# Whole float32 scores in twelve heads instead of eight, and the high parts of V cast on ACT instead of GpSimd

## The chip, the cores and the metric

The kernel runs on one core of one Trainium2 chip. The metric is the device time of one execution in microseconds (us). The engines are named as the profile names them: PE is TensorE's matmul, PEld its weight load, DVE is VectorE, ACT is ScalarE, POOL is GpSimd, and SP issues the transfers.

## The reference

Eight batches of eight heads of attention (576 positions, 64 columns a head) with a mask in blocks of 64 positions, then a mixer: a product of rank 32 along the sequence added to the input, and a feed-forward layer of 512 to 2048 to 512 with a residual.

```python
scores = scale * np.matmul(q, k.transpose(0, 1, 3, 2))
mask = block_i >= block_j
scores = np.where(mask, scores, -1000000000.0)
scores = scores - np.max(scores, axis=-1, keepdims=True)
attn = np.exp(scores)
attn = attn / (np.sum(attn, axis=-1, keepdims=True) + 1e-09)
out = np.matmul(attn, v)
...
h = xt @ U @ V
u = x + h.transpose(0, 2, 1)
ch = np.maximum(u @ w_ch1, 0.0) @ w_ch2
return u + ch
```

All inputs and the output are float32.

## The kernel before

The 64 heads (number h, batch h // 8) pass through the same steps one after the other. `split_qk` fetches q and k of a head into a tile `raw` of 128 partitions: 64 hold q and k, and the other 64 hold a pattern that brings the mask into the product. `softmax` makes the scores of five row tiles (the last, 128 rows by 576 columns, in a double bank `bw`; the others in single banks), takes the row maximum on DVE (L949) and the exponential on ACT (L960). `normalise` multiplies by the inverse of the row sums on POOL (L986). `transpose` turns the probabilities on PE (L1019) and moves them out of PSUM, `apply_v` multiplies by V, and after every second head `mix` does the product of rank 32 and writes u to DRAM.

Two ways of computing stand beside each other, and a constant says how many heads go the first way.

- Scores. The first `FS` = 8 heads are whole: ACT scales k (L874), and one float32 product of `raw` with itself (L931) gives scores and mask. PE runs such a product at float32, and it shows as two MATMUL records each in the trace. The other heads are split: ACT casts q and k to float32r, a type whose products PE runs faster (L877 and L878), POOL and DVE form the rests (L880, L885), SP copies the high part of q into a second tile (q<-q, L892) and fetches q and k a second time into the other 64 partitions (L861), and two float32r products (L935, L936) are summed. In the last two of the whole heads DVE also copies the mask's pattern into the tiles of the split heads (L867).
- Probabilities times V. The first `FP` = 10 heads multiply in float32 (L1061). The others split probabilities and V into high and low parts (L996, L1038 and `split_v`) and multiply in float32r (L1077). In `split_v` POOL makes the high part (L904), then the low one (L907).

The weights of the feed-forward layer arrive as 64-bit words that ACT, DVE and POOL turn into float32 and split (`split64`, L331 to L361); this work is laid beside heads 0 to 17 or so. As soon as the first batch is through `mix`, the feed-forward products with the first half of the hidden columns (`ffn_chunk`, L465 and L488) fill PE between the steps of attention, in two banks `bf` of their own. After the last head they run alone, and the second half of the hidden columns follows (`block_products`, L659).

The order on each engine is made ahead of time: `Plan.issue` plays the tasks with an estimated cost each. A task has an engine, a cost in ns, a priority (a head's number times 1000 and a little more; filler has 1,000,000 and more), and the buffers that it reads and writes. Of the tasks whose inputs are there, the one with the lowest number is issued. Tasks on POOL and those marked `port` are never planned at the same time. What is issued stays in that order on its engine. A change of one cost, engine or task thus lays the whole order anew.

Of the kernel before, what the change touches and what calls it, by code (L numbers as in the profile page):

```python
# [13 lines left out]
ALU = mybir.AluOpType  # L14
# [29 lines left out]

FP = 10

FS = 8

PB = (1, 1, 1, 2, 2)

# [87 lines left out]
class Plan:  # L138
# [8 lines left out]
    def add(self, engine, ns, prio, fn, reads=(), writes=(), hold=(), after=0, port=False):  # L147

        n = len(self.tasks)
        deps = set()  # L150
        for b in reads:
            deps.update(b.writers)
            b.readers.append(n)
        for b in hold:
            deps.update(b.readers, b.writers)
        for b in writes:
            deps.update(b.readers, b.writers)
            b.writers, b.readers = [n], []
        deps.discard(n)
        slots = {b for b in (*reads, *writes) if b.pool is not None}  # L160
        for b in slots:
            b.users += 1
        self.tasks.append((engine, ns, prio, fn, deps, after, slots, port or engine == "POOL"))
# [76 lines left out]
def _act(n, sbuf=False):  # L240
    return (93 if sbuf else 52) + 0.833 * n
# [13 lines left out]
def attention_then_mixer(  # L255
# [10 lines left out]
    nc = tc.nc  # L266
# [10 lines left out]
    def f32(ap):  # L277
        return ap.bitcast(F32)
# [525 lines left out]
    for r in raw_r:  # L804
# [3 lines left out]
        for x, fill in ((qi, 1.0), (ki, NEG)):  # L808
            nc.gpsimd.affine_select(
                out=x[:, :, 1, :], in_=x[:, :, 1, :], pattern=[[-1, 4], [0, 64]], compare_op=ALU.not_equal,  # L810
# [44 lines left out]
    def split_qk(h, pr):  # L855
        raw, q1, k1, q2, k2 = (r[h % 2] for r in (raw_r, q1_r, k1_r, q2_r, k2_r))

        def fetch():
            nc.sync.dma_start(out=raw[0:64, :], in_=qk[h])
            if h >= FS:  # L860
                nc.sync.dma_start(out=raw[64:P, :], in_=qk[h])  # L861

        if h in (FS - 2, FS - 1):

            for n, (x, o) in enumerate(((q2, 0), (k2, S))):
# [3 lines left out]
                )  # L869
        add("SP", 1640 if h >= FS else 820, pr, fetch, writes=[raw], after=DL)  # L870
        if h < FS:
            add(
# [21 lines left out]
    def split_v(h, pr):  # L894
        s = h % 2
        raw, vs = vr_r[h // 2 % 2], vs_r[s]
        if s == 0:
            add("SP", 910, pr, lambda: nc.sync.dma_start(out=raw.ap, in_=v[h // 2]), writes=[raw], after=DL)
        if h < FP:
            return  # L900
        hi, lo = vs[:, :, 0:64], vs[:, :, 64:P]
        add(
            "POOL", 430, pr,
            lambda: nc.gpsimd.tensor_scalar(out=hi, in0=raw[:, s], scalar1=1.0, scalar2=1.0, op0=ALU.mult, op1=ALU.mult),  # L904
            [raw], [vs],
        )
        add("POOL", 820, pr, lambda: nc.gpsimd.tensor_sub(lo, raw[:, s], f32(hi)), [raw, vs], [vs])  # L907

    def softmax(h, tiles, pr):
# [14 lines left out]
        def products():  # L924
            for i, at in parts:
                qs = slice(P * i + 64 - (P if i else 64), P * i + 64)
                for j in range(2 if wide else 1):
                    o = bank[:, j, :T] if wide else view(i, at)
                    ks = slice(j * T, j * T + T) if wide else slice(0, P * i + 64)
                    if h < FS:  # L930
                        nc.tensor.matmul(  # L931
# [7 lines left out]
        for i in tiles:  # L939
            ns += [T] * 4 if wide else [P * i + 64] * 2  # L940
            ms += [P if i else 64] * (4 if wide else 2)
        if h < FS:
            add("PE", sum(1.667 * n for n in ns) / 2, pr, products, [raw], [bank])
# [207 lines left out]
    wa = weight_tiles(wp, 0)  # L1151
    split_qk(0, 0.0)
    split_v(0, 0.1)
    mixing_weights(MP)
    wab = weight_bufs()
    load_w1(lambda: wa, 0, wab, lambda n: WP0 + WP1 * n, (0,))
    for h in range(NH):
        pr = 1000.0 * h
        if h + 1 < NH:
            split_qk(h + 1, max(pr - LA, 1.0))  # L1160
        for g, tiles in ((1, (4, 3)), (0, (2, 1, 0))):
            for x in ((4,), (3,)) if g else ((2,), (1, 0)):
                softmax(h, x, pr + 10)
            normalise(h, tiles, pr + 10)
        for g in (1, 0):
            for part in range(2):
                transpose(h, g, part, pr + 20 + 10 * (1 - g))
            apply_v(h, g, pr + 30)
        if h + 1 < NH:
            split_v(h + 1, pr + 1000)  # L1170
        if h % 2 == 1:
            mix(h // 2, pr + 40)
        if h == min(WH, NH - 1):
            gate = Buf()
            gate.writers = [len(plan.tasks) - 1]
            load_w2(lambda: wa, 0, wab, lambda n: WPB + WP1 * n, [gate], ks=range(FH))
            load_w1(lambda: wa, 0, wab, lambda n: WP2 + WP3 * n, (1,), [gate])
            load_w2(lambda: wa, 0, wab, lambda n: WP4 + WP3 * (n - FH), [gate], ks=range(FH, FC))
# [59 lines left out]
```

## Time and profile before

| | |
|---|---|
| median of 3 runs | 1201.78 us (1198.8 to 1202.18) |
| the profiled execution | 1201.04 us |
| its span | 1199.2 us |
| PE, DVE, ACT, POOL busy | 1169.1, 980.7, 734.0, 426.3 us |
| first split product of scores (L935), last | 77.3 us, 659.4 us |
| first filler product (L465) | 103.5 us |

The span is what lies between the first and the last instruction of the profile. In a row of a timeline the first number is the start and the second the duration, in us from the span's start; in a group, busy time and mean duration stand before the second bar and the idle time ahead of its instructions, with what ended it, behind it. PE's matmuls are pipelined: the next one starts before the one before it ends, so a stretch of work is read from start to start.

### The profile page before, as it was taken

The page shows a single profiled execution, that of the slowest core. Times are in us where ns is not written, and L with a number is a line of the kernel's source. Part 1 is how long each engine was busy: PE and PEld are TensorE (multiplying, and loading weights), DVE is VectorE, ACT ScalarE, POOL GpSimd, SP SyncE. Part 2 cuts the span into 40 slices and gives each one's busy share as a digit, 9 for nine tenths or more (in the row PEclk, how much of TensorE's full clock was granted, in tenths as well). Part 3 has the DMA queues.
Part 4 walks back from the last instruction along what each step waited for, and adds up shares of the span by engine and source line. Part 5 has one row for each costly group of instructions (what it writes and reads, how often), then busy time and mean ns, then how long its engine had stood idle before and what let it go on. Part 6 is the DMA issues. An engine that isn't in the chain of part 4 may idle for free.

```text
span 1199.2 us, 25106 instructions
## 1 busy us (share of the span) xinstructions
PE 1169.1 (97%) x8970; PEld 1123.6 (94%) x8970; DVE 980.7 (82%) x2061; ACT 734.0 (61%) x1822; POOL 426.3 (36%) x588
## 2 busy tenths in 40 slices
PE   7989998999999999999999999999999999999998
PEld 5657888999999999999999999999999999999998
DVE  6879899888988898888887488425989889889887
ACT  6878686777878787878786344213544544544443
POOL 4558766665656566665654112210000000000000
PEclk9999999999999999999999999999999999999999
DMA  4465656535364535354532343211231231231221
GB/s 127 146 172 155 188 166 166 139 97 156 81 171 108 144 104 153 101 158 106 144 98 70 104 147 111 81 54 49 72 119 49 72 119 49 72 119 60 60 80 40
DMA packets 76428, 132.13 MB, mean 110 GB/s; under 512 B 9040, under 2 KB 53072, under 8 KB 76304
## 3 DMA queue, kind: packets, MB, share of 16 engines
q1 hardware_dynamic: 76304, 130.53, 38.8%
q8 instruction: 71, 1.16, 0.4%
q14 instruction: 53, 0.43, 0.1%
HBM read 92.75 MB, written 29.49 MB: 102 GB/s over the span
## 4 chain that ended last, share of the span: by engine, by line
PE 79%; DVE 11%; ACT 4%; issue 2%; DMA 2%; SPq 0%; POOL 0%; ACTq 0%; DVEq 0%; POOLq 0%
PE bb L659 29%; PE bf L465 10%; PE bf L488 10%; PE ba L1019 7%; PE ba L1077 5%; PE bg L465 4%; PE bg L488 4%; DVE mx L949 2%; DVE pl L1038 2%; ACT p L960 2%; PE ba L935 2%; PE ba L936 2%; PE ba L1061 1%; PE ba L1116 1%; PE ba L1102 1%
## 5 line engine op out<-in xcount | busy, mean ns | idle before, releaser
L986 POOL TENSOR_SCALAR p<-p,rv 128x192 f32<-128x192 f32 (+4 forms) x320 | 181.0, 580 | 150.5 <-DVE rv L977 92.7
L659 PE MATMUL bb<-hh,w1l 128*128 128x288 f32 x704 | 170.1, 295 | 0.0
L659 PE MATMUL bb<-hh,w1h 128*128 128x288 f32 x704 | 169.4, 295 | 0.0
L960 ACT ACTIVATE p<-ba,mx 128x448 f32<-128x448 f32 (+3 forms) x248 | 114.3, 466 | 22.2 <-DVE mx L949 18.9
L1019 PE MATMUL ba<-ident,p 128*128 128x128 f32 x768 | 123.5, 275 | 2.2 <-DVE pw L994 0.7
L1038 DVE TENSOR_TENSOR pl<-ba,ph 128x512 fp32r<-128x512 f32 x216 | 114.0, 550 | 11.7 <-ACT ph L996 9.2
L659 PE MATMUL bb<-hl,w1h 128*128 128x288 f32 x576 | 123.0, 295 | 0.1
L659 PEld LDWEIGHTS bb<-hh,w1l 128*128 128x128 f32 x704 | 122.9, 190 | 0.0
L659 PEld LDWEIGHTS bb<-hh,w1h 128*128 128x128 f32 x704 | 121.9, 188 | 0.0
L488 PE MATMUL bf<-hh,w2h 128*128 128x288 f32 x392 | 121.2, 309 | 0.0
L488 PE MATMUL bf<-hl,w2h 128*128 128x288 f32 x392 | 116.4, 297 | 0.0
L488 PE MATMUL bf<-hh,w2l 128*128 128x288 f32 x392 | 115.6, 295 | 0.0
L996 ACT CAST ph<-ba 128x512 fp32r<-128x512 f32 x216 | 100.5, 493 | 23.1 <-PE ba L1019 18.3
L447 POOL TENSOR_TENSOR ul<-ur,uh 128x288 fp32r<-128x288 f32 x72 | 63.3, 907 | 129.7 <-PE bf L465 72.6
L613 ACT CAST hh<-hb 128x576 fp32r<-128x576 f32 x98 | 65.9, 672 | 60.6 <-PE bb L659 58.1
L949 DVE TENSOR_REDUCE mx<-ba 128x1 f32<-128x448 f32 (+3 forms) x248 | 94.1, 407 | 10.0 <-PE ba L936 5.4
L1019 PEld LDWEIGHTS ba<-ident,p 128*128 128x128 f32 x768 | 90.5, 141 | 7.9 <-issue 4.5
L880 POOL TENSOR_TENSOR q<-raw,q 64x576 fp32r<-64x576 f32 x56 | 82.6, 1475 | 29.1 <-issue 9.2
L659 PEld LDWEIGHTS bb<-hl,w1h 128*128 128x128 f32 x576 | 91.9, 188 | 0.4 <-DVE hl L614 0.4
L1077 PE MATMUL ba<-ph,vs 128*128 128x256 f32 (+3 forms) x432 | 90.7, 263 | 0.1
L465 PE MATMUL bf<-uh,w1l 128*128 128x288 f32 x392 | 80.8, 303 | 0.0
L488 PEld LDWEIGHTS bf<-hh,w2l 128*128 128x128 f32 x392 | 74.9, 191 | 0.2
(167 smaller groups left out, 3288.1 us busy)
## 6 DMA issues: line engine op xcount, KB each, us to landing
raw<-in_qk_dram SPq DMA_DIRECT2D x120, 288.0 KB, 4.4
st<-in_w_dram SPq DMA_DIRECT2D x32, 512.0 KB, 3.6
o_d<-ot SPq DMA_DIRECT2D x72, 144.0 KB, 2.1
vr<-in_v_dram SPq DMA_DIRECT2D x32, 320.0 KB, 3.4
ur<-u_d SPq DMA_DIRECT2D x64, 144.0 KB, 3.0
whole<-o_d SPq DMA_DIRECT2D x32, 288.0 KB, 3.2
out_dram<-whole SPq DMA_DIRECT2D x32, 288.0 KB, 2.2
ur<-u_d SPq DMA_DIRECT2D x30, 288.0 KB, 3.2
```

Source lines behind the costliest of these rows:

```text
L465: nc.tensor.matmul(ps[:, :T], w()[wn][:, k, fs], m[k].ap, start=(i == 0), stop=(i == len(ops) - 1))
L488: nc.tensor.matmul(ps[:, :T], w()[wn][:, f, ms], hs[f][x].ap, start=(i == 0), stop=(i == len(ops) - 1))
L613: add("ACT", _act(2 * T, True), E, lambda: nc.scalar.copy(h.ap, x[0]()), [x[1]], [h])
L659: nc.tensor.matmul(bank[:, i, :T], x()[:, w(k)], p.ap[:, k, :], start=first and n == 0, stop=last and n == len(ops) - 1)
L880: "POOL", 1380, pr, lambda: nc.gpsimd.tensor_sub(q1[64:P, :], raw[64:P, 0:S], f32(q1[64:P, :])),
L949: lambda i=i, at=at: nc.vector.tensor_reduce(out=mx[: P if i else 64, i : i + 1], in_=view(i, at), op=ALU.max, axis=AX.XY if wide else AX. ...
L960: nc.scalar.activation(out.rearrange("p (j k) -> p j k", j=2) if wide else out, view(i, at), AF.Exp, bias=mx[:rows, i : i + 1], accum_out= ...
L986: lambda x=x, rows=rows, i=i: nc.gpsimd.tensor_scalar(out=x, in0=x, scalar1=rv[:rows, i : i + 1], scalar2=1.0, op0=ALU.mult, op1=ALU.mult),
L996: add("ACT", _act(n), pr, lambda: nc.scalar.copy(out(), inp()), reads, writes)
L1019: nc.tensor.transpose(out=bank[:, a : a + P], in_=pt_r[i][h % PB[i]][:, j * P : (j + 1) * P], identity=perm.ap)
L1038: "DVE", _dve(m), pr, lambda: nc.vector.tensor_sub(pl[:, low], bank[:, :m], f32(ph[:, low])), [bank, bh], [bl]
L1077: nc.tensor.matmul(bank[0 : c.stop, a:n], vs[:, j, c], x[:, _at(g, j)], start=(i == 0), stop=(i == len(ops) - 1))
```

## The change

`FS` becomes 12: heads 8 to 11 too compute their scores in one whole float32 product. For these four heads the casts L877 and L878, the rests L880 and L885, the copy L892 and the second fetch L861 fall away, and the scaling L874 comes in. The copies of the pattern (L867) move from heads 6 and 7 to heads 10 and 11. The row tile 3 of these heads' scores stays in the attention's own banks, since that choice goes by h < 8 and not by `FS`.

In `split_v` the high part of V is made by ACT (`nc.scalar.copy`, a cast to float32r) with a planned cost of `_act(320, True)`, 93 + 0.833 x 320 = 360 ns, in place of POOL's multiplication by one with 430 ns. This goes for the 54 heads from 10 to 63. The low part stays on POOL.

```diff
@@ -44,7 +44,7 @@
 FP = 10
 
-FS = 8
+FS = 12
 
@@ -900,8 +900,7 @@
         hi, lo = vs[:, :, 0:64], vs[:, :, 64:P]
         add(
-            "POOL", 430, pr,
-            lambda: nc.gpsimd.tensor_scalar(out=hi, in0=raw[:, s], scalar1=1.0, scalar2=1.0, op0=ALU.mult, op1=ALU.mult),
+            "ACT", _act(320, True), pr, lambda: nc.scalar.copy(hi, raw[:, s]),
             [raw], [vs],
         )
         add("POOL", 820, pr, lambda: nc.gpsimd.tensor_sub(lo, raw[:, s], f32(hi)), [raw, vs], [vs])
```

## The prediction

> **What bounds the kernel now.** I read the page first for the engine that is never free, then busy time by stretches of the span for where that engine is idle after all, and last the waits and the order of time in those stretches. On the page:
>
> ```profile
> span 1199.2 us, 25106 instructions
> PE 1169.1 (97%) x8970; PEld 1123.6 (94%) x8970; DVE 980.7 (82%) x2061; ACT 734.0 (61%) x1822; POOL 426.3 (36%) x588
> ```
>
> TensorE (PE) is busy in 1169.1 of 1199.2 us, 30.1 us short of the span. Attention has the higher priority, and the feed-forward products (L465, L488) fill what it leaves, so an attention step that gets slower merely hands its place on TensorE to filler. The time can move in two ways only: by the work given to TensorE, or by its idle time. Where that lies (columns: length; busy time and instructions of PE, PEld, DVE, ACT, POOL; granted clock; DMA share; GB/s):
>
> ```profile
> 10.00:66.00 56.00, 53.83 (x294) 36.03 (x293) 46.33 (x122) 45.71 (x130) 28.91 (x43) 1.00 0.48 138
> 66.00:104.00 38.00, 31.45 (x198) 22.38 (x197) 29.21 (x62) 30.81 (x84) 23.91 (x28) 1.00 0.64 168
> 104.00:200.00 96.00, 87.03 (x665) 82.09 (x664) 89.62 (x205) 71.27 (x196) 66.86 (x83) 0.95 0.59 166
> 200.00:660.00 460.00, 457.05 (x3777) 445.67 (x3777) 391.76 (x1017) 360.16 (x1032) 277.18 (x397) 1.00 0.47 124
> 122.00:128.00 6.00, 4.48 (x21) 4.26 (x22) 4.05 (x9) 1.68 (x5) 3.04 (x3) 0.72 0.31 102
> 178.00:186.00 8.00, 5.73 (x23) 4.58 (x24) 7.67 (x13) 3.98 (x11) 4.19 (x6) 0.57 0.61 176
> ```
>
> Idle TensorE by difference: 2.2 us of 56 while heads 0 to 7 run (4%); 6.5 us of 38 in 66-104, where heads 8 to 10 have split scores and no filler is ready yet; 9.0 us of 96 in 104-200, where DVE is 93% busy; 2.9 us of 460 after that. In two places the granted clock sinks too: 4.48 us of work at 0.72 and 5.73 at 0.57 cost 1.3 and 2.5 us, so 104-200 holds 12.7 us that could be had. The change touches the second and third rows.
>
> **The change part by part: the scores of heads 8 to 11.** Each gets one whole product in place of two split ones. TensorE in the order of time (start, duration), first a whole head, then a split one; the matmuls are pipelined, so the price is from a row's start to the next row's start:
>
> ```profile
> 49.62 1.39 PE L931 MATMUL ba<-raw 128*128 128x320 f32 x6
> 50.84 2.04 PE L1061 MATMUL ba<-pw,vr 128*64 128x256 f32 x10
> ...
> 53.93 1.14 PE L931 MATMUL bw<-raw 128*128 128x288 f32 x4
> 54.90 0.92 PE L931 MATMUL bf<-raw 128*128 128x448 f32 x2
> 55.65 0.27 PE L1102 MATMUL ba<-ident,xt 128*64 128x128 f32 x1
> ...
> 102.44 0.47 PE L935 MATMUL ba<-k,q 128*128 128x448 f32 x1
> ...
> 103.54 0.77 PE L465 MATMUL bf<-uh,w1h 128*128 128x288 f32 x4
> ...
> 105.78 0.38 PE L935 MATMUL bw<-k,q 128*128 128x288 f32 x1
> ...
> 106.39 0.70 PE L465 MATMUL bf<-uh,w1h 128*128 128x288 f32 x4
> ```
>
> Whole: 1.22 (50.84 - 49.62) + 0.97 + 0.75 = 2.94 us. Split: 1.10 + 0.61 = 1.71 us. That is 1.23 us more a head and **+4.9 us** for four, on the path because TensorE has no room elsewhere (4.6 to 5.2 if the starts are each off by a slot of 0.1).
>
> What leaves the other engines, by lines (duration in ns, lowest/median/highest):
>
> ```profile
> L877 ACT CAST q<-raw x56: 656/673/693, 69.4 to 630.6; 128x576 fp32r<-128x576 f32 x56
> L878 ACT ACTIVATE k<-raw x56: 667/686/711, 69.9 to 631.9; 128x576 fp32r<-128x576 f32 x56
> L880 POOL TENSOR_TENSOR q<-raw,q x56: 1396/1426/1993, 70.5 to 633.9; 64x576 fp32r<-64x576 f32 x56
> L885 DVE SCALAR_TENSOR_TENSOR k<-raw,k x56: 718/752/1910, 70.7 to 633.4; 64x576 fp32r<-64x576 f32 x56
> L874 ACT ACTIVATE raw<-raw x8: 669/682/686, 4.5 to 55.2; 64x576 f32<-64x576 f32 x8
> L892 SPq DMA_DIRECT2D q<-q x56: 482/489/1835, 72.3 to 636.4; - x56
> ```
>
> A head gives up two ACT passes for one (-0.68 us), 1.43 us of GpSimd, 0.75 of DVE, and on SP's queue the copy q<-q (L892) and the second fetch of q and k (L861). All of this runs beside TensorE, so it is worth nothing in itself. It counts in 66-104 through the waits:
>
> ```profile
> PE bw L936 <- DMA q<-q: 3.1, 1, 3.1
> 72.34 8.43 DMA q<-q
> DMA to landing us min/median/max: 2.3/3.0/8.4
> ```
>
> The first split head cannot start its second product until q<-q has landed, 8.4 us after issue, and TensorE stands for 3.1 us with nothing to fill. After the change this place belongs to a whole head. TensorE's order at head 8, before:
>
> ```order
> L1019 MATMUL ba_96<-ident,p_1_140 128x128 x2
> L935 MATMUL bw<-k_0_147,q_0_145 128x288
> L936 MATMUL bw<-k_0_128,q_0_126 128x288
> ```
>
> and in the changed program (it is a line shorter from L903 on, so L930 is the whole product, L934 and L935 the split one); first head 8, then, at "...", head 12, now the first split one:
>
> ```order
> L1101 MATMUL ba_96<-ident,xt_163 64x128
> L930 MATMUL bw<-raw_130 128x288 x2
> L1018 MATMUL ba_97<-ident,p_1_138 128x128
> ...
> L465 MATMUL bf_91<-ul_112,w1h_199 128x288
> L465 MATMUL bf_91<-ul_113,w1h_199 128x288
> L934 MATMUL bw<-k_0_147,q_0_145 128x288
> L935 MATMUL bw<-k_0_128,q_0_126 128x288
> ```
>
> Head 8 no longer needs a copy, and head 12 comes behind filler. I take 66-104 at the pace of the whole heads before it, 4% idle: 1.5 us in place of 6.5, **-5.0 us**. At best nothing stays idle (-6.5); at worst only the wait for q<-q goes (-3.1). The two casts a head of L867 (the rows that split heads reuse) move from heads 6 and 7 to 10 and 11; DVE has 8.8 us free in 66-104 and hides four casts of 1 us:
>
> ```profile
> L867 DVE CAST q<-raw x2: 685/1029/1373, 32.9 to 41.2; 64x576 fp32r<-64x576 f32 x2
> ```
>
> Without that cover the 4 us would come before the row maxima of heads 10 and 11, inside the worst case above.
>
> **The high parts of V.** 54 instructions go from GpSimd to ACT:
>
> ```profile
> L904 POOL TENSOR_SCALAR vs<-vr 128x320 fp32r<-128x320 f32 x54 | 24.8, 460 | 54.7 <-PE ba L1077 51.3 <-DMA raw<-in_qk_dram 2.0 <-ACT uh L445 0.6
> L445 ACT CAST uh<-ur 128x288 fp32r<-128x288 f32 x72 | 27.7, 432 | 2.8 <-PE bf L465 1.8 <-DVE ur L1136 0.6 <-PE bg L465 0.2
> L360 ACT CAST w1h<-z x8: 600/618/622, 32.5 to 131.5; 128x512 fp32r<-128x512 f32 x8
> L960 ACT ACTIVATE p<-ba,mx 128x448 f32<-128x448 f32 (+3 forms) x248 | 114.3, 466 | 22.2 <-DVE mx L949 18.9 <-DVE xt L1085 0.7 <-DVE rv L976 0.6
> ```
>
> ACT casts 288 columns in 0.432 us and 512 in 0.618, so 320 take about 0.46, 24.8 us in all, what GpSimd gives up. ACT is at 78% in 200-660 (360.16 of 460); some 46 casts (one in 10 us) add 21 us, 83%. That is cover enough for 0 on TensorE; bounds -1 and +3 us (its idle time there gone, or doubled). The cast waits for the P V products two heads back (L1077), and ACT's exponentials queue behind it. The changed order on ACT, at one of these casts (L1082 takes the product out of PSUM, L903 is the cast):
>
> ```order
> L1118 COPY tb_169<-ba_98 32x128
> L1082 COPY tmp_162<-ba_96 64x320
> L1120 CAST t_0_167<-tz_168 32x128
> L903 CAST vs_151<-vr_149 128x5x64
> L353 ACTIVATE z_103<-st_101 128x512
> ```
>
> The cast stands behind a copy that already waits for the last product reading that V, so it hardly adds a wait of its own.
>
> In 104-200 the lateness is DVE's, and some comes with GpSimd's work:
>
> ```profile
> L331 DVE TENSOR_SCALAR z<-z x36: 175/423/2499, 8.5 to 757.7; 128x512 f32<-128x512 f32 x32, 96x288 f32<-96x288 f32 x2, 128x128 f32<-128x128 f32 x1, 128x32 f32<-128x32 f32 x1
> 180.60 2.50 DVE L331 TENSOR_SCALAR z<-z 128x512 f32<-128x512 f32 x1
> 180.20 0.45 POOL L904 TENSOR_SCALAR vs<-vr 128x320 fp32r<-128x320 f32 x1
> 181.34 0.86 POOL L907 TENSOR_TENSOR vs<-vr,vs 128x320 fp32r<-128x320 f32 x1
> PE ba L1131 <- DVE xt L1085: 1.7, 1, 1.7
> ```
>
> An operation with a median of 0.42 us took 2.50 while GpSimd ran back to back, L904 among it, in the stretch where the clock sank. Some eight L904 leave this stage, 3.7 us of such meetings, and attention comes to it about one head further on. The order is laid out anew, though, so stalls may fall elsewhere. I take **-3 us** of the 12.7, a little less than the 3.7; bounds -12.7 (all) and +4.8 (one more stretch like 178-186: 2.3 idle and 2.5 of clock).
>
> [...]
>
> Sum: 4.9 - 5.0 - 3 + 0 = **-3.1 us**. The profiled execution took 1201.04 us (span 1199.2); the median of the runs is 0.7 above it, so the forecast is 1201.04 - 3.1 = 1197.9, and 1198.7 against the median; I give **1198.3**. All bounds together are -17.6 to +9.9.
>
> **The rivals.**
> *The stalls of 104-200 go.* If 9 of their 12.7 us vanish: 4.9 - 5.0 - 9 = -9.1, about 1192. For it: DVE works less and GpSimd's meetings fall. Against: DVE stays over 90%, since the weights still have to be split in this stage.
> *A draw.* The 66-104 gain pays for the heavier products and nothing else changes: 4.9 - 5.0 = -0.1, about 1201. For it: the two terms rest on the best rows; against: nothing says that the old stalls would come back unchanged.
> *Slower: the switch to split heads stalls at head 12.* The copy q<-q is late there too, since SP has fetches, weights and the filler's traffic in one queue: 3.1 us of wait and 2.5 of sunk clock: 4.9 - 5.0 + 3.1 + 2.5 = +5.5, about 1206.5. It decides once the copy lands later than the filler ahead of head 12 lasts. Against: 18 filler products stand shortly ahead of it in TensorE's order, and this copy took 3.0 us to land in the median.
>
> ACT's other exponentials, and TensorE's longest wait for them:
>
> ```profile
> L960 ACT ACTIVATE p<-bw,mx 128x576 f32<-128x576 f32 x64 | 47.5, 742 | 16.9 <-DVE mx L949 15.5 <-DVE rv L976 0.5
> PE ba L1019 <- ACT p L960: 2.8, 5, 1.4
> ```
>
> *ACT blocks.* The 51.3 us that L904 waited on GpSimd come to ACT's queue. Of ACT's own waits for the row maxima (18.9 + 15.5) TensorE saw 2.8 us, a twelfth; a twelfth of 51.3 is 4.2: -3.1 + 4.2 = +1.1, about 1202. [...]
>
> **How the numbers follow.** Forecast 0.42, stalls gone 0.15, draw 0.23, head 12 0.13, ACT 0.07. A measurement here can tell about 0.3% (3.6 us) from no change, so faster means under 1198.2. The forecast lies on that line: I give 0.23 of its 0.42 to faster and 0.19 to same, and 0.04 of the draw to faster. Faster 0.23 + 0.15 + 0.04 = 0.42; same 0.19 + 0.17 + 0.05 = 0.41; slower 0.13 + 0.02 (draw) + 0.02 (ACT) = 0.17. The range for 8 in 10 is 1191 to 1206, which takes in four of the cases and the near side of the slower one; the likeliest case alone has 1195 to 1201.
>
> **What would show it.** Right: idle TensorE in 66-104 under 2 us, no wait for q<-q at head 8, twelve heads of L930 at 2.9 us each, first filler no later than the 103.5 us of before, ACT at 83% in 200-660 with TensorE's idle time there still near 3 us. Wrong: a wait for q<-q or for the split k at head 12, waits of ACT on the P V products at L903, more idle time or more low clock in 104-200 than 12.7 us together, or 66-104 not above 92% busy.

## The result, and the profile after

The changed kernel takes 1188.71 us in the median of four runs (1185.44 to 1190.97), the kernel before, on the same chip, 1201.82 (1198.8 to 1202.18): a ratio of 0.989 with a 95% interval of 0.9859 to 0.992. That is 13.1 us less, where 3.1 us less was forecast (against the 1201.04 of the profiled execution), and 2.3 us below the lower end of the range. The profiled execution took 1186.6 us. Two of the four runs, the profiled one among them, took 1185.44 and 1186.6 us at a mean granted clock of 1.000, the other two 1190.83 and 1190.97 us at 0.997, so what the profile shows is the quicker kind.

The page of the changed kernel, its span and busy times:

```profile
span 1184.8 us, 25065 instructions
PE 1168.3 (99%) x8970; PEld 1120.7 (95%) x8970; DVE 967.7 (82%) x2057; ACT 750.6 (63%) x1872; POOL 392.3 (33%) x530
```

TensorE's idle time fell from 30.1 to 16.5 us (1184.8 - 1168.3): 13.6 of the 14.4 us by which the span is shorter. By stretches, in the columns of before (length; busy time and instructions of PE, PEld, DVE, ACT, POOL; granted clock; DMA share; GB/s):

```profile
10.00:66.00 56.00, 54.81 (x305) 37.05 (x304) 44.74 (x118) 47.41 (x134) 30.63 (x45) 1.00 0.43 129
66.00:104.00 38.00, 35.18 (x198) 23.20 (x197) 34.28 (x75) 31.02 (x85) 21.86 (x29) 1.00 0.50 147
104.00:200.00 96.00, 94.07 (x745) 89.01 (x745) 88.14 (x217) 79.67 (x222) 61.23 (x76) 1.00 0.65 183
200.00:660.00 460.00, 459.11 (x3805) 448.43 (x3804) 385.40 (x1008) 373.88 (x1073) 254.16 (x351) 1.00 0.45 119
```

| | idle PE before | idle PE after | gain |
|---|---|---|---|
| 10-66 | 2.2 | 1.2 | 1.0 |
| 66-104 | 6.5 | 2.8 | 3.7 |
| 104-200 | 9.0 | 1.9 | 7.1 |
| 104-200, the sunk clock | 3.7 | 0 | 3.7 |
| 200-660 | 2.9 | 0.9 | 2.0 |

In 104-200 DVE works about as long as before (88.1 for 89.6 us) and GpSimd 5.6 us less, but TensorE gets through 745 matmuls in place of 665. What became of the place where the clock sank is seen in the filler there. Of the products L488 alone, in 175-190 (length, PE busy, clock, DMA share, GB/s), first before, then after:

```profile
175.00:190.00 15.00, 0.04 (x1) 0.77 0.49 140
```

```profile
175.00:190.00 15.00, 7.27 (x48) 1.00 0.64 184
```

Before, the filler had run dry: for 15 us TensorE had nothing but the steps of attention. The filler needs the weight tiles (the weights come as 64-bit words, the other inputs as float32), and the last one is split by GpSimd at L361 (start, duration). Before, it was done at 189.7 us and L488 came back at 190; after, it was done at 174.9:

```profile
187.89 1.82 POOL L361 TENSOR_TENSOR w2l<-z,w2h 128x512 fp32r<-128x512 f32 x1 [0.16 <-ACT w2h L360]
```

```profile
173.61 1.30 POOL L361 TENSOR_TENSOR w2l<-z,w2h 128x512 fp32r<-128x512 f32 x1 [5.19 <-ACT w2h L360]
```

The heads are ahead by 10 to 21 us: the row maximum (L949 before, L948 after) of head 9 starts at 79 us in place of 89, of head 16 at 161 in place of 173, of head 21 at 212 in place of 233. The waits of TensorE for other engines, the three longest of the whole span, and the cast that is new on ACT:

```profile
PE bw L930 <- ACT raw L874: 6.2, 2, 5.4
PE ba L1018 <- ACT pw L995: 1.3, 2, 0.8
PE ba L1018 <- DVE tz L1119: 1.2, 2, 0.7
...
L903 ACT CAST vs<-vr x54: 449/459/472, 88.6 to 634.4; 128x320 fp32r<-128x320 f32 x54
  POOL vs L906: 61.1, 21
```

The first is the start of the kernel and was there before (6.0). There is no wait for q<-q any more, at head 8 or at head 12. The cast takes the 0.46 us that were worked out. ACT never waits for it; GpSimd does, for 61.1 us in all, and the profile lists no wait of TensorE for GpSimd.

### The profile page after: what moved, and what is told of

Same layout as the page of the kernel before. It is cut to its first block, busy times and chain, and to the rows that moved or that the text cites. A ratio compares the mean times of both kernels' runs of the same rounds, so it can differ in the third digit from the quotient of the medians.

```text
span 1184.8 us, 25065 instructions
## 1 busy us (share of the span) xinstructions
PE 1168.3 (99%) x8970; PEld 1120.7 (95%) x8970; DVE 967.7 (82%) x2057; ACT 750.6 (63%) x1872; POOL 392.3 (33%) x530
## 3 DMA queue, kind: packets, MB, share of 16 engines
q8 instruction: 71, 1.16, 0.4%
## 4 chain that ended last, share of the span: by engine, by line
PE 83%; DVE 8%; ACT 5%; issue 2%; DMA 2%; POOL 1%; SPq 0%; ACTq 0%; DVEq 0%; POOLq 0%
PE bb L659 30%; PE bf L465 11%; PE bf L488 9%; PE ba L1018 7%; PE ba L1076 6%; PE bg L488 4%; PE bg L465 4%; PE ba L1060 2%; PE ba L934 2%; DVE pl L1037 2%; PE ba L935 2%; ACT p L959 2%; PE ba L1101 1%; PE ba L1115 1%; PE ba L930 1%
## 5 line engine op out<-in xcount | busy, mean ns | idle before, releaser
L959 ACT ACTIVATE p<-ba,mx 128x448 f32<-128x448 f32 (+2 forms) x248 | 114.7, 468 | 19.3 <-DVE mx L948 15.8
L1037 DVE TENSOR_TENSOR pl<-ba,ph 128x512 fp32r<-128x512 f32 x216 | 114.9, 549 | 12.7 <-ACT ph L995 11.0
L488 PE MATMUL bf<-hh,w2h 128*128 128x288 f32 x384 | 119.4, 311 | 0.0
L488 PE MATMUL bf<-hl,w2h 128*128 128x288 f32 x384 | 113.5, 296 | 0.0
L488 PE MATMUL bf<-hh,w2l 128*128 128x288 f32 x384 | 112.7, 294 | 0.0
L948 DVE TENSOR_REDUCE mx<-ba 128x1 f32<-128x448 f32 (+3 forms) x248 | 94.5, 407 | 11.9 <-PE ba L935 6.7
L659 PEld LDWEIGHTS bb<-hl,w1h 128*128 128x128 f32 x576 | 91.9, 188 | 0.4 <-DVE hl L614 0.4
L880 POOL TENSOR_TENSOR q<-raw,q 64x576 fp32r<-64x576 f32 x52 | 74.9, 1440 | 30.4 <-issue 16.6
L465 PE MATMUL bf<-uh,w1l 128*128 128x288 f32 x392 | 78.7, 301 | 0.0
L1076 PEld LDWEIGHTS ba<-ph,vs 128*128 128x128 f32 x432 | 73.1, 189 | 2.4 <-DVE pl L1037 1.2
```

The costliest lines, as they stand in the source:

```text
L465: nc.tensor.matmul(ps[:, :T], w()[wn][:, k, fs], m[k].ap, start=(i == 0), stop=(i == len(ops) - 1))
L488: nc.tensor.matmul(ps[:, :T], w()[wn][:, f, ms], hs[f][x].ap, start=(i == 0), stop=(i == len(ops) - 1))
L659: nc.tensor.matmul(bank[:, i, :T], x()[:, w(k)], p.ap[:, k, :], start=first and n == 0, stop=last and n == len(ops) - 1)
L880: "POOL", 1380, pr, lambda: nc.gpsimd.tensor_sub(q1[64:P, :], raw[64:P, 0:S], f32(q1[64:P, :])),
L948: lambda i=i, at=at: nc.vector.tensor_reduce(out=mx[: P if i else 64, i : i + 1], in_=view(i, at), op=ALU.max, axis=AX.XY if wide else AX. ...
L959: nc.scalar.activation(out.rearrange("p (j k) -> p j k", j=2) if wide else out, view(i, at), AF.Exp, bias=mx[:rows, i : i + 1], accum_out= ...
```

## The experiments

Two theories stood against each other. Theory F: whole scores in heads 8 to 11 take work from ACT, DVE, GpSimd and SP, so heads and weight tiles come earlier, the filler no longer runs dry at 175-190, and the clock has no reason to sink. (The texts below also call the whole scores alone theory S, and the move of V alone theory V.) Theory O: each change lays the order of all engines anew, and the 13 us are a lucky order. A third question was what the move of V to ACT does by itself. In the tables the ratio is to the kernel before on the same chip; idle and clock are TensorE's.

### The two halves of the change

Only the first line of the change, the kernel before otherwise:

```diff
-FS = 8
+FS = 12
```

> One part alone: FS = 12, the high parts of V stay on GpSimd. If the whole scores give the gain (theory S): idle TensorE in 66-104 falls from 6.5 to about 3 us and in 104-200 from 9.0 to 2-4 us with the clock at 1.00, and the time is -8 to -13 us against before (about 1190). If the move of V gives it (theory V): 66-104 improves as said, the 4.9 us of heavier products are paid, 104-200 keeps 7 to 11 us idle and a clock of 0.95, and the time is within 3 us of before. If the order that happens to be laid out decides (theory O), anything from -10 to +5 us, in 104-200 alone.

Only the second, the changed kernel with eight whole heads:

```diff
-FS = 12
+FS = 8
```

> The other part alone: ACT makes the high parts of V, FS stays 8. Theory V: 104-200 loses its stalls (idle from 9.0 to 2-3 us, clock 1.00) and the time is -7 to -10 us; 66-104 stays at 6.5 us idle with the wait for q<-q. Theory S: 104-200 keeps 6 to 10 us idle, time within 3 us of before. Theory O: anything from -10 to +5 us, in 104-200 alone.

| | us | ratio | interval | idle 66-104 | idle 104-200, clock |
|---|---|---|---|---|---|
| before | 1201.5 | | | 6.5 | 9.0, 0.95 |
| whole scores alone | 1192.94 | 0.9928 | 0.9912-0.9944 | 3.3 | 3.0, 1.00 |
| ACT for V alone | 1205.17 | 1.0037 | 1.002-1.0054 | 4.6 | 7.4, 0.98 |
| both | 1188.71 | 0.989 | 0.9859-0.992 | 2.8 | 1.9, 1.00 |

With the whole scores alone 104-200 reads nearly as after the change; with ACT for V alone the stall of 180-190 stays, if smaller (before, TensorE was busy for 7.36 us there at 0.74). The first row is of the whole scores alone, 104-200, the second of ACT for V alone, 180-190:

```profile
104.00:200.00 96.00, 93.01 (x749) 89.71 (x748) 89.61 (x216) 74.97 (x209) 63.31 (x82) 1.00 0.64 177
```

```profile
180.00:190.00 10.00, 8.65 (x52) 7.57 (x53) 7.91 (x19) 8.13 (x23) 5.86 (x7) 0.83 0.53 151
```

So most of the gain comes with the scores. ACT for V cost 3.7 us with eight whole heads and brought 4.2 with twelve (1192.94 to 1188.71, where the two intervals still overlap). But each of these kernels also has an order of its own, so the engine was changed once more under an order that stays. In the first kernel the plan takes the cast for ACT's, as in the changed kernel, and the instruction goes to GpSimd; in the second the plan takes it for GpSimd's, as before, and the instruction goes to ACT. The planned order of all other instructions stays.

```diff
# the changed kernel, planned for ACT
-            "ACT", _act(320, True), pr, lambda: nc.scalar.copy(hi, raw[:, s]),
+            "ACT", _act(320, True), pr, lambda: nc.gpsimd.tensor_scalar(out=hi, in0=raw[:, s], scalar1=1.0, scalar2=1.0, op0=ALU.mult, op1=ALU.mult),
# the kernel before, planned for POOL
-            lambda: nc.gpsimd.tensor_scalar(out=hi, in0=raw[:, s], scalar1=1.0, scalar2=1.0, op0=ALU.mult, op1=ALU.mult),
+            lambda: nc.scalar.copy(hi, raw[:, s]),
```

> The changed kernel, laid out as if ACT made the high parts of V (so every engine's order of everything else is unchanged, row for row), but the 54 instructions are issued on GpSimd, as before the change. If the move to ACT has a worth of its own beyond the order (GpSimd's meetings with DVE, its queue), this kernel is slower than after by 3 us or more: 1192 and above, with more idle TensorE in 104-200 than after's 1.9 us. If only the order counts and the engine does not matter, it stays within 2 us of after, 1187 to 1191, GpSimd 25 us busier and ACT 25 us less.

> The kernel before (eight heads with whole scores), laid out as if GpSimd made the high parts of V (every engine's order of everything else unchanged, row for row), but the 54 instructions are issued on ACT. The layout is then that of before, not the one that the move to ACT got in the second run (1205.2). If the engine is worth something by itself: 1198 or below, by fewer slow DVE operations in 104-200. If the engine does not matter: 1199.5 to 1203.5. If ACT's queue suffers (casts of V that stand where GpSimd had room, ahead of exponentials): 1204 or above, with waits of TensorE for ACT.

The changed order with GpSimd took 1186.98 us (ratio 0.9886, 0.987 to 0.9903), which the 0.989 of the change itself does not differ from. The order of before with ACT took 1207.48 (1.0055, 1.0036 to 1.0074): slower. In 200-660 the first does as many matmuls as after, the second 55 fewer than the 3777 before:

```profile
200.00:660.00 460.00, 458.17 (x3810) 448.81 (x3809) 387.07 (x1013) 361.04 (x1035) 275.93 (x396) 1.00 0.45 119
```

```profile
200.00:660.00 460.00, 454.46 (x3722) 438.49 (x3721) 384.71 (x1001) 370.27 (x1063) 255.84 (x350) 1.00 0.45 121
```

So under the changed order the engine that makes the high parts of V brought nothing by itself, and in an order that was not laid out for it the cast on ACT cost some 7 us. There GpSimd waited 69.1 us for it (second row; the group's idle time stands behind the second bar):

```profile
L904 ACT CAST vs<-vr 128x320 fp32r<-128x320 f32 x54 | 24.7, 458 | 0.0
L907 POOL TENSOR_TENSOR vs<-vr,vs 128x320 fp32r<-128x320 f32 x54 | 47.8, 886 | 79.3 <-ACT vs L904 69.1 <-DMA ur<-u_d 4.1 <-PE ba L936 3.1
```

After the change it waits 61.1 us as well and nothing comes of it, so that wait alone does not explain the 7 us. Nor do the waits for ACT that were expected: TensorE's waits for the exponentials (L960) came to 3.8 us in all, and to 3.0 before. Through which step it reaches TensorE stays open.

### How much the order alone is worth

Other planned costs for the same instruction lay the order anew and change nothing else. From the kernel before (430 ns), with eight whole heads:

```diff
-            "POOL", 430, pr,
+            "POOL", 360, pr,
```

> The kernel before with no work changed: only the planned cost of GpSimd's high part of V is 360 instead of 430 ns, so the order on the engines is laid anew from about head 11 on (104 us). Theory O: the time moves by 4 us or more in one direction or the other, and idle time and low clock in 104-200 differ by that much from the 9.0 us and 3.7 us of before. Theories S and V: within 3 us of before, 7 to 11 us idle in 104-200.

and with 520 in its place:

> As the run with 360, with 520 ns planned. Theory O: 4 us or more away from before or from the run with 360. Theories S and V: within 3 us of both, 7 to 11 us idle in 104-200.

From the changed kernel (360 ns) with twelve whole heads, to 301 and to 443 ns, and the same 443 ns with eight whole heads:

```diff
-            "ACT", _act(320, True), pr, lambda: nc.scalar.copy(hi, raw[:, s]),
+            "ACT", _act(250, True), pr, lambda: nc.scalar.copy(hi, raw[:, s]),
```

> The changed kernel with no work changed: the planned cost of ACT's high part of V is 301 instead of 360 ns, so the order is laid anew from about head 10. Theory S or F: 1185 to 1193, like the changed kernel. Theory O: the changed kernel's 1188.7 is one lucky order, and this one lies above 1195.

> As the run with 301, with 443 ns planned. Theory S or F: 1185 to 1193. Theory O: above 1195.

> Eight heads with whole scores and ACT for the high parts of V, as in the second run, with another planned cost of the move, 443 ns in place of 360, so that the order falls out otherwise. It adds a layout to the family with eight heads, which so far lies at 1199.7 to 1207.8. Theory (the number of whole heads sets the family, the order scatters by 4 us): 1199 to 1208, with a low clock in 180-190. Rival (the twelve-head kernels were lucky in their order, and so could one of eight be): below 1195.

| whole heads, V on, planned ns | us | ratio | interval | idle 104-200, clock |
|---|---|---|---|---|
| 8, POOL, 360 | 1207.77 | 1.0055 | 1.0038-1.0071 | 10.5, 0.95 |
| 8, POOL, 520 | 1199.67 | 0.9992 | 0.9977-1.0008 | 9.3, 0.96 |
| 8, ACT, 443 | 1201.63 | 1.0011 | 0.9996-1.0026 | 7.5, 0.96 |
| 12, ACT, 301 | 1196.74 | 0.997 | 0.9955-0.9985 | 3.6, 1.00 |
| 12, ACT, 443 | 1187.92 | 0.9895 | 0.9871-0.9919 | 1.9, 1.00 |

With those above there are six kernels of eight whole heads, 1199.7 to 1207.8, mean 1204, and five of twelve, 1187.0 to 1196.7, mean 1191. The order alone moves a kernel by 4 to 6 us to either side, so theory O is right in part: the change's own 13 us could as well have been 5. The kernel planned with 301 ns came to 1196.74, where its expectation had put theory O (above 1195). But the medians of the two families do not overlap (the nearest are 1196.74 and 1199.67; single executions of these two do), and the place where they differ is the same each time: 104-200 has 7.4 to 10.5 us idle at a clock of 0.95 to 0.98 in every kernel of eight, 1.4 to 3.6 us at 1.00 in every kernel of twelve. The slice 180-190 of three orders with eight heads (430 to 360; 430 to 520; ACT with 443), one fence each:

```profile
180.00:190.00 10.00, 5.75 (x27) 5.49 (x27) 7.11 (x13) 3.91 (x12) 7.51 (x9) 0.71 0.36 102
```

```profile
180.00:190.00 10.00, 6.51 (x32) 5.56 (x32) 7.76 (x23) 6.80 (x20) 6.45 (x11) 0.66 0.48 127
```

```profile
180.00:190.00 10.00, 7.70 (x46) 6.88 (x46) 7.68 (x15) 8.00 (x22) 5.31 (x6) 0.80 0.39 113
```

The slowest of the twelve (301 ns) loses elsewhere too: in the profiled execution, which at 1200.75 us was the slowest of its ten, the clock sinks in 66-104:

```profile
66.00:104.00 38.00, 34.13 (x180) 22.71 (x179) 31.25 (x69) 28.52 (x78) 18.96 (x26) 0.91 0.47 134
```

### The weight tiles, earlier and later

Theory F says that the stall follows the last weight tiles. Their due times are constants of the plan. First the kernel before with the tiles due earlier, then the changed kernel with the tiles due later:

```diff
# the kernel before
-WP2, WP3, WP4 = 9000.0, 1000.0, 13000.0
+WP2, WP3, WP4 = 8000.0, 800.0, 11200.0
# the changed kernel
-WP2, WP3, WP4 = 9000.0, 1000.0, 13000.0
+WP2, WP3, WP4 = 10500.0, 1000.0, 16000.0
```

> The kernel before with one line of priorities changed: the splitting of the weights of the second part (L331 to L361) is due one to two heads earlier (WP2, WP3, WP4 = 8000, 800, 11200 instead of 9000, 1000, 13000). Theory F (filler runs out): in before the filler stopped at 175.0 us and came back at 190.0, right after the last weight tile was split (189.7), and TensorE stood and lost clock in between. With the tiles earlier the stretch 170-190 is busy (idle under 1.5 us instead of 4.9, clock 1.00) and the time falls by 4 to 8 us. Theory O (only the order laid out decides): no rule for 170-190, time anywhere from -5 to +6 us. Theory S (the whole scores as such): within 3 us of before.

> The changed kernel with the second part of the weights due later (10500, 1000, 16000): the last tile comes one head later than in either kernel. Theory F: the stall of before comes back, at 185-205 us: 3 us or more of idle TensorE and a clock under 1.00, and the time is 4 to 9 us above the changed kernel's 1188.7. Theory S: within 3 us of 1188.7. Theory O: from -3 to +8 us without that place.

Earlier tiles: 1208.31 us (1.0068, 1.0042 to 1.0095). The last tile starts at 165.59, TensorE is full in 170-180 (7.70 of 10 before), and the clock no longer sinks in 104-200. But 170-190 still has 2.6 us idle, where under 1.5 was expected, and the time rose by 8 us where a fall of 4 to 8 was expected: now the clock sinks in 66-104, where the tiles' work meets heads 8 to 10.

```profile
165.59 1.27 POOL L361 TENSOR_TENSOR w2l<-z,w2h 128x512 fp32r<-128x512 f32 x1 [2.58 <-ACT w2h L360]
...
66.00:104.00 38.00, 29.48 (x166) 21.38 (x165) 29.65 (x69) 29.57 (x81) 22.88 (x25) 0.91 0.63 177
...
170.00:180.00 10.00, 10.00 (x87) 9.67 (x85) 8.96 (x22) 8.58 (x26) 6.71 (x10) 1.00 0.73 189
180.00:190.00 10.00, 7.43 (x58) 6.79 (x57) 9.73 (x20) 4.75 (x14) 6.57 (x9) 1.00 0.40 119
```

Later tiles: 1211.29 us (1.0097, 1.0066 to 1.0129), 22.6 us above the change. The last tile starts at 193.02, and the stall is back in the kernel with twelve whole heads, larger than before. Expected were only 4 to 9 us above the change; the excess is also in 66-104 (4.9 us idle, 2.8 after the change) and in 200-660 (6.7, 0.9 after):

```profile
193.02 1.28 POOL L361 TENSOR_TENSOR w2l<-z,w2h 128x512 fp32r<-128x512 f32 x1
...
104.00:200.00 96.00, 86.95 (x642) 81.01 (x641) 84.83 (x193) 71.70 (x201) 58.12 (x72) 0.93 0.59 162
...
180.00:190.00 10.00, 7.71 (x39) 6.66 (x38) 8.89 (x21) 7.41 (x20) 5.15 (x8) 0.67 0.48 113
```

At 170-190 the clock goes as theory F says in both, though neither time was forecast well, and each also has a new order. The rest of the record bears the theory out. The longest pause between two filler products (L465 and L488, start to start) in 150-200, beside the ends of two weight tiles, in us:

| kernels | fifth of the eight w1l tiles done | last w2l tile done | longest pause | filler back after the last tile |
|---|---|---|---|---|
| six of eight whole heads | 99.2-102.2 | 182.2-189.7 | 9.0-15.3 | 0.3-3.8 |
| five of twelve | 87.3-91.9 | 169.7-179.8 | 3.8-4.7 | |
| eight, tiles earlier | 94.3 | 166.9 | 3.0 | |
| twelve, tiles later | 88.3 | 194.3 | 16.4 | 2.1 |

Each kernel whose last tile came after 182 us had the long pause, which ended just behind that tile, and none of the others had it, nor did ten, fourteen and sixteen whole heads (last tile at 176.2 or earlier, pauses of 4.2 at most). The first experiment also shows that these earlier due times do not pay with eight whole heads: the tiles' work then meets the heads in 66-104. In the kernels of twelve the tiles come earlier already there, with the same due times. That the whole scores make this room follows from these rows; twelve heads with the earlier tiles were not run.

### Ten, fourteen and sixteen whole heads

Would more whole heads bring more, or fewer as much? The changed kernel with other counts, and sixteen also with the planned cost of 443 ns:

```diff
-FS = 12
+FS = 16
```

> The changed kernel with whole scores in sixteen heads in place of twelve (heads 12 to 15 too); the order is laid out anew. The theory so far: heads 8 to 11 gained because they ran before the filler was there and because ACT, DVE and GpSimd got further ahead; in heads 12 to 15 filler already covers their waits and TensorE idles for only 1.9 us in all of 104-200, so four more heads can only add their 4 x 1.23 = 4.9 us of products: about 1193 to 1194, with the spread of a new order of 4 us either way; TensorE busy 4 to 6 us longer than after. Rival (relief of the other engines is what pays, wherever it is): the waits left over, 16.5 us of idle TensorE in all, fall by 5 us or more and the time stays at 1189 or below.

> The changed kernel with whole scores in ten heads. Eight (with ACT) took 1201.6 to 1207.5, twelve 1186.6 to 1196.7. Mechanism (heads 8 to 11 run while no filler is ready; each that is whole saves waits there and brings the later stages forward): about half way, 1193 to 1199, with a smaller sink of the clock in 170-190 than with eight heads. Order (luck): anything from 1187 to 1208, not between.

> The changed kernel with whole scores in fourteen heads. With sixteen, TensorE was busy for 7.9 us more than with twelve (2.0 us a head) and idle for 5.9 us more. Mechanism (heads 12 and up run beside filler, so a whole head only adds its products): half way between 1188.7 and 1201.7, 1192 to 1198, TensorE 3 to 5 us busier than after. Order (luck): outside that.

> Sixteen whole heads with the other planned cost of the cast of V (443 ns in place of 360), so that the order falls out otherwise. Mechanism: again 1197 to 1206, TensorE busy 1173 to 1178 us. If the 1201.7 of sixteen heads was its order: below 1194.

| whole heads | us | ratio | interval | PE busy | idle 66-104, clock | idle 104-200 | idle 200-400 |
|---|---|---|---|---|---|---|---|
| 10 | 1205.47 | 1.003 | 1.0013-1.0047 | 1174.0 | 6.4, 0.96 | 5.0 | 5.9 |
| 12, the change | 1188.71 | 0.989 | 0.9859-0.992 | 1168.3 | 2.8, 1.00 | 1.9 | 0.6 |
| 14 | 1197.18 | 0.9966 | 0.9951-0.9981 | 1172.2 | 4.3, 1.00 | 2.6 | 2.6 |
| 16 | 1201.71 | 1.001 | 0.9996-1.0024 | 1176.2 | 4.2, 1.00 | 3.5 | 2.0 |
| 16, 443 ns | 1203.78 | 1.0018 | 1.0003-1.0033 | 1177.4 | 3.4, 1.00 | 2.5 | 2.1 |

Above twelve the time rises with the count (fourteen in one order only), and both orders of sixteen agree: TensorE is busy for 2.0 to 2.3 us more a head (1.23 by the slots of the prediction) and idle for some 6 to 8 us more as well. The forecast for sixteen, 1193 to 1194, was 8 us too low; the one for fourteen held. Below twelve the expectation failed: ten is not half way but as slow as eight, with the stall at 170-190 nearly gone and new ones in 66-104 and 200-400. One thing that sets ten and eight apart from the rest is where the switch from whole to split heads falls. It lasts 16 to 30 us in these kernels, from the row maximum of the last whole head to that of the first split one. TensorE over that time with 8 (before), 10, 12, 14 and 16 whole heads, one fence each:

```profile
62.00:82.00 20.00, 14.94 (x91) 10.05 (x90) 14.01 (x29) 15.87 (x42) 12.79 (x16) 1.00 0.79 190
```

```profile
84.00:108.00 24.00, 20.99 (x124) 14.38 (x123) 20.13 (x40) 17.12 (x46) 16.25 (x17) 1.00 0.68 177
```

```profile
103.00:119.00 16.00, 15.83 (x118) 14.13 (x117) 13.19 (x37) 13.91 (x42) 8.34 (x11) 1.00 0.66 174
```

```profile
128.00:147.00 19.00, 17.81 (x144) 16.62 (x143) 17.28 (x40) 15.63 (x43) 12.39 (x15) 1.00 0.84 226
```

```profile
145.00:174.00 29.00, 28.04 (x211) 24.99 (x209) 26.52 (x64) 22.53 (x62) 19.08 (x24) 1.00 0.62 168
```

It leaves TensorE idle for 5.1 and 3.0 us where no filler is there yet, and for 0.2 to 1.2 us where it is. The first filler comes at about the same time in all, after the change at

```profile
L465 PE MATMUL bf<-uh,w1h x16: 292/296/399, 104.6 to 117.0; 128*128 128x288 f32 x16
```

Twelve is the smallest of these counts whose switch falls almost wholly behind it. By these rows that is worth some 3 to 5 us, though no run tries it by itself; the rest of the step from ten to twelve, the 5.9 us in 200-400 above all, was seen in one order of ten only and is not settled. Of all these kernels none beats the change by more than the runs can tell.

## Why the prediction was wrong

The direction was right and the size was not: the time is 2.3 us below the range. The direction was in part luck, since the first two terms cancel (4.9 - 5.0) and the whole forecast hung on the -3 for 104-200, whose cause was wrong. By its steps, measured in the two profiled spans (-14.4 us in all; the sunk clock is an estimate, busy time x (1 - clock)):

- **Heads 8 to 11, +4.9.** TensorE's busy time, with the 3.7 us of sunk clock taken off before, went from 1165.4 to 1168.3: +2.9. The whole products kept their price: in the groups of the changed kernel twelve heads take 44.4 us of records, 3.7 a head, and eight took 30.3 before (11.7 + 10.4 + 8.2 in the same three groups), 3.8 a head. Kernels with the same products differ by up to 4.4 us in busy time (see the last section), so the +2.9 does not refute the 4.9.

```profile
L930 PE MATMUL ba<-raw 128*128 128x320 f32 (+3 forms) x80 | 20.9, 372 | 0.0
L930 PE MATMUL bw<-raw 128*128 128x288 f32 x48 | 15.2, 442 | 6.3 <-ACT raw L874 6.2
L930 PE MATMUL bf<-raw 128*128 128x448 f32 x16 | 8.3, 601 | 0.0
```

- **66-104, -5.0.** -3.7. The wait for q<-q is gone, and head 12 has none, so the rival that put it there fell. The 4% of idle time taken from the heads before was 7% here. Two signs of the prediction failed: idle under 2 us here (2.8), and the first filler no later than 103.5 (104.6).
- **The high parts of V, 0.** Zero under the changed order with either engine. The 83% of ACT in 200-660 came out at 81% (373.88 of 460), and TensorE's idle time there fell by 2.0 instead of staying. The rival in which ACT blocks does not show here; the order of before with ACT in it shows that the move can cost 7 us, though not that it does so by this rival's queue.
- **104-200, -3. This is the step that failed.** It was -10.8: 7.1 us of idle time and all 3.7 of the clock. The prediction took GpSimd's L904, which meets DVE there, for what could be taken away, and priced eight meetings. That was the wrong cause: with L904 back on GpSimd under the same order 104-200 has 1.4 us idle and the clock at 1.00, and DVE's L331 still shows durations up to 2.2 us after the change. The largest part, 6.3 us (4.0 idle, 2.3 of clock), lies in 175-190, and what stood behind it was the filler, dry for want of the last weight tiles. Another 2.8 (1.5 idle, 1.3 of clock) is the stall of 122-130, where TensorE waited 1.7 us for DVE (L1131 for L1085). That part goes with the order rather than with the scores: four of the five other kernels of eight whole heads keep the clock at 1.00 in 104-130. The prediction never asked why TensorE had no filler in 175-190, where it should have had some. It even says that attention comes to the stage about a head further on; it did not carry that on to the weight tiles, whose numbers in the plan stand among those of the heads. The rival "the stalls of 104-200 go" had the price, -9, with a chance of 0.15.
- **The draw** fell with this step: the old stalls did not come back.
- **Not in the sum:** -1.0 in 10-66, which comes with the whole scores (1.1 to 1.3 us idle in all five kernels of twelve, 2.1 to 2.9 in all six of eight), and -2.0 in 200-660, which comes with the order (0.9 to 5.9 in the five, 1.5 to 6.2 in the six).
- **The range.** The best bounds add up to -15.6 (4.6 - 6.5 - 1 - 12.7), not to the -17.6 that the prediction gives; that is 1185.4, and the lower end of 1191 left it out, though the result lies inside it. The measured spread of the order alone, 4 to 6 us to either side, is most of the range's own half (7.5); of it the prediction priced one more stretch of stall, on the slower side.

Together: 2.9 - 3.7 - 10.8 - 2.0 - 1.0 = -14.6, beside the span's -14.4.

## What to carry to other kernels

Where filler hides the waits of a chain, ask of each stall first why no filler stood there: what the filler lacks (here a weight tile, made by the same engines that the chain keeps busy) can be worth more than the wait that shows. Where every change lays a whole order anew, price that as well, by a few kernels that differ in a planned cost alone; and try an engine for an operation under a fixed order before crediting the engine. A switch from one way of computing to another seems to cost least where other work is ready to cover it; that rests on five kernels here, not on a test of its own.

## What the runs showed of the hardware that was not expected

In the slices below the granted clock falls to 0.50, for 6.8 us at a wait of 3.47 us and for 3.4 us at one of 1.7. Two-microsecond slices of TensorE in the kernel with the later tiles (length, PE busy, clock, DMA share, GB/s), and then of the kernel before:

```profile
174.00:176.00 2.00, 1.18 (x12) 1.00 0.27 108
176.00:178.00 2.00, 0.00 (x0) 0.91 0.00 0
178.00:180.00 2.00, 1.35 (x5) 0.50 0.48 141
180.00:182.00 2.00, 2.00 (x11) 0.50 0.94 221
182.00:184.00 2.00, 2.00 (x11) 0.50 1.09 289
184.00:186.00 2.00, 1.75 (x12) 0.89 0.08 13
```

```profile
118.00:120.00 2.00, 2.00 (x20) 1.00 0.43 139
120.00:122.00 2.00, 1.80 (x15) 1.00 0.76 258
122.00:124.00 2.00, 0.48 (x2) 0.94 0.03 12
124.00:126.00 2.00, 2.00 (x8) 0.50 0.12 44
126.00:128.00 2.00, 2.00 (x13) 0.71 0.77 251
```

In the first case TensorE stood for 3.47 us, in the second for 1.7. The clock then stays at half although TensorE is full again, and a full slice holds 8 to 11 matmuls in place of 20 (118-120). A slice at 0.91 has had 0.36 of its 2 us at half, so the first fall lasts 0.36 + 6 + 0.44 = 6.8 us and the second, by the same working, 0.24 + 2 + 1.16 = 3.4. The second stall thus cost about twice itself, 1.7 us of standing and half of 3.4, and that is how an estimated 3.7 us of the gain came without an instruction being saved.

The length of one wait does not tell whether the clock falls. In the kernel before, its start and end left out, the clock changes at 123.75, 127.17, 178.37 and 185.19, with 3.42, 51.20 and 6.82 us between, which is 1, 15 and 2 times 3.41. Stretches of that length, laid along these times, show (length, PE busy, clock, DMA share, GB/s):

```profile
75.97:79.38 3.41, 1.71 (x19) 1.00 1.10 217
79.38:82.79 3.41, 1.97 (x10) 1.00 0.94 205
120.34:123.75 3.41, 1.69 (x13) 1.00 0.36 117
123.75:127.17 3.42, 3.42 (x14) 0.50 0.33 98
174.96:178.37 3.41, 2.10 (x15) 1.00 0.24 54
178.37:181.78 3.41, 1.95 (x8) 0.50 0.82 245
181.78:185.19 3.41, 3.11 (x15) 0.50 0.57 159
185.19:188.60 3.41, 2.00 (x14) 1.00 0.23 47
```

The wait of 3.1 us for q<-q reaches from the first of these stretches into the second, and the clock stayed at 1.00. The wait of 1.7 us lies inside the third, and at its end the clock fell. The busy time of a stretch does not tell it either: the clock fell behind stretches busy for 1.69 and 2.10 us and stayed at 1.00 behind those busy for 1.71, 1.97 and 2.00. What makes it fall is not shown.

Busy time is no measure of the work done here either. The six kernels of eight whole heads do the same products, yet TensorE is busy for 1169.1 to 1173.5 us, and it is not the sunk clock alone: the one with the highest clock of them in 104-200 (ACT for V alone, 0.98) has 1171.5, the kernel before, at 0.95, has 1169.1. In 200-660, at a clock of 1.00, the order of before with ACT has 122 ns of busy time a matmul (454.46 / 3722), the changed kernel 120.7 (459.11 / 3805), though the two need not hold the same mixture of products there. Whether the records hide short gaps was not tested; the count of matmuls in a stretch, beside its busy time, says more of the work than the busy time alone.
